# A pad of 128 bytes at the right end of SBUF in a fused attention and two-layer kernel

## Chip, cores and metric

The kernel runs on one core of one Trainium2 chip. The metric is the time of one execution on the device in microseconds. Where several executions were timed, the median stands with the lowest and the highest.

## What is computed

Three steps follow each other. The attention works over the channels (256 by 256 scores for each of 2 batches), so that its product with `v` can be folded into the weights of the next layer. Two feed-forward layers follow, with 1536 and 2048 hidden units, over 12032 tokens of 256 channels, all in float32.

```python
B, N, C = (2, 6016, 256)
qn = q / (np.linalg.norm(q, axis=1, keepdims=True) + 1e-06)
kn = k / (np.linalg.norm(k, axis=1, keepdims=True) + 1e-06)
s = kn.transpose(0, 2, 1) @ qn / tau
a = softmax(s)                       # over the last axis, plus 1e-9 in the sum
x = (v @ a).reshape(B * N, C)
x = (sigmoid(x @ w_gate) * (x @ w_val)) @ w_out      # 256 -> 1536 -> 256
h = x @ w_in                                         # 256 -> 2048
return (h - np.tanh(h)) @ w_out2                     # 2048 -> 256
```

## The kernel before

Every float32 operand is kept as two halves, a rounded high part and the rest (`split`, line 91), and each product is three matmuls: high by high, high by low, low by high (`prod`, line 415, whose matmuls are lines 419, 420 and 421). The first operand of a matmul is the weight that is loaded into the array (128 by 128), the second is the data that stream through it (up to 512 columns).

At the start the scores of batch 0 are summed up over all its rows (lines 324 to 346), while a side stream converts the first layer's weights from a raw layout (`convert`, line 95: load, three steps on VectorE, a rescaling on GpSimd, a cast on ScalarE, a subtraction). After the softmax, `aw_block` (line 285) multiplies the attention matrix into these weights; the result is `aw`. From then on a list of units, sorted by hand-set due times (lines 632 to 641), is run in order. A unit of the first layer (`s1_mm`, line 426) makes gate and value `ps` from `vhl` and `aw`; its second half (`part_c`, line 501) adds `y` from `hl` and `wo`. A unit of the second layer (`s2_mm`, line 448) makes `h` from `yhl` and `wi`, and its second half adds `o` from `hl` and `wv`. The tokens are cut into 24 tiles: 22 of 512 and 2 of 384, the last of each batch. The scores of batch 1 are computed in between by a list of side steps (line 625).

SBUF is filled from both ends by pools that open and close like a stack on each side. On the left lie `base` (constants, `wo`, `aw`), `vp` (`vraw`, `vhl`), then `sp` for the attention of batch 0, and after `sp` is closed `mp` (`yhl`, `sg`, `hl`), `cst` or later `m2` and `cst2` (staging of the other weights, and the second layer's work tiles), `qp`, `qp2` and `yp`. On the right lie `wp` (line 81: the six `wgv` tiles) and `stg` (line 82: raw tiles and `x` tiles of their conversion); both are closed in turn, and `w2p` (line 406) takes the place with eight `wi` and eight `wv` tiles. The pools have `reuse_waits="tile"`: a new tile waits for the users of just those old tiles whose bytes it takes.

The places that matter here, in bytes of a partition, as the layout of the kernel before has them:

| tiles | side | from | to | start modulo 512 |
|---|---|---|---|---|
| `ident`, `ones` | left | 16512 | 17536 | 128 |
| `wo` (6 of 4096) | left | 17632 | 42208 | 224 |
| `aw` (6 of 8192) | left | 42208 | 91360 | 224 |
| `vhl` | left | 95456 | 103648 | 224 |
| `sp`, all | left | 103648 | 153944 | 224 for its large tiles |
| `yhl`, in `mp` | left | 103648 | 111840 | 224 |
| `hl` (4 of 4096), in `mp` | left | 115936 | 132320 | 224 |
| last tiles of `cst` | left | 148704 | 156896 | 224 |
| last tiles of `cst2`, `qp`, `qp2` | left | 150752 | 163064 | 224 for the large ones |
| `stg`: raw tiles from 155616, 159712, 163808, 167904, then `x` tiles | right | 155616 | 180192 | 480 |
| `wp`: `wgv` (6 of 8192) | right | 180192 | 229344 | 480 |
| `w2p`: `wi`, `wv` (16 of 4096) | right | 163808 | 229344 | 480 |

All slices of these tiles that TensorE reads begin a multiple of 512 bytes after the tile's start.

Of the kernel before, what the change touches and what calls it, by code (L numbers as in the profile page):

```python
# [8 lines left out]
F32 = mybir.dt.float32  # L9
# [8 lines left out]
P = 128  # L18
# [39 lines left out]
def attn_moe_kernel(  # L58
# [18 lines left out]
    pp = ctx.enter_context(tc.tile_pool(name="pp", bufs=1, space=bass.MemoryType.PSUM))  # L77
    sctx, wctx, gctx, cctx = ExitStack(), ExitStack(), ExitStack(), ExitStack()
    vp = ctx.enter_context(tc.tile_pool(name="vp", bufs=1))
    sp = sctx.enter_context(tc.tile_pool(name="sp", bufs=1, reuse_waits="tile"))  # L80
    wp = wctx.enter_context(tc.tile_pool(name="wp", bufs=1, side="right", reuse_waits="tile"))
    stg = gctx.enter_context(tc.tile_pool(name="stg", bufs=1, side="right", reuse_waits="tile"))
# [450 lines left out]
    def side_load(r):  # L533
        if r < R:
            raw = qp.tile([P, 2, D], F32, tag="raw", bufs=2, name=f"raw1_{r}")
            for t, src in ((0, q), (1, k)):
                nc.sync.dma_start(raw[:, t, :], token_rows(src, 1)[:, r, :])
            q1["raw", r] = raw
# [86 lines left out]
    side = [side_open, lambda: side_load(0), lambda: side_load(1)]  # L625
# [105 lines left out]
```

## Time and profile before

| | us |
|---|---|
| median of 3 runs | 2364.32 |
| lowest and highest | 2363.01 and 2366.67 |
| the profiled execution's own time | 2363.61 |
| its span, first to last instruction | 2361.7 |
| TensorE busy in it | 2325.5 |

Some 1.9 us of the profiled execution lie outside the span. Times in the rows below are counted from the span's start. Matmuls overlap: the duration of one (about 390 ns for 512 columns) is longer than the distance from one start to the next, and it is this distance that sets the pace.

### The profile page before, as it was taken

The page shows a single profiled execution, that of the slowest core. Times are in us where ns is not written, and L with a number is a line of the kernel's source. Part 1 is how long each engine was busy: PE and PEld are TensorE (multiplying, and loading weights), DVE is VectorE, ACT ScalarE, POOL GpSimd, SP SyncE. Part 2 cuts the span into 40 slices and gives each one's busy share as a digit, 9 for nine tenths or more (in the row PEclk, how much of TensorE's full clock was granted, in tenths as well). Part 3 has the DMA queues.
Part 4 walks back from the last instruction along what each step waited for, and adds up shares of the span by engine and source line. Part 5 has one row for each costly group of instructions (what it writes and reads, how often), then busy time and mean ns, then how long its engine had stood idle before and what let it go on. Part 6 is the DMA issues. An engine that isn't in the chain of part 4 may idle for free.

```text
span 2361.7 us, 28761 instructions
## 1 busy us (share of the span) xinstructions
PE 2325.5 (98%) x10704; PEld 1953.9 (83%) x10704; DVE 1870.5 (79%) x2917; ACT 1563.2 (66%) x2808; POOL 118.3 (5%) x82
## 2 busy tenths in 40 slices
PE   8899999999999999999999999999999999999998
PEld 8777888888888888878889888888888888888887
DVE  7898787888888888888777778777787777777777
ACT  4456667676677766677666666666666666666667
POOL 4531000000000000000000000000000000000004
PEclk9999999999999999999999999999999999999999
DMA  8530000101101001000110000000000000000000
GB/s 296 217 116 18 28 18 27 36 14 36 36 19 36 22 33 36 18 16 27 63 54 1 16 18 1 18 18 1 18 10 10 18 10 10 18 1 16 10 1 16
DMA packets 37516, 81.53 MB, mean 35 GB/s; under 512 B 3840, under 2 KB 17152, under 8 KB 35840
## 3 DMA queue, kind: packets, MB, share of 16 engines
q1 hardware_dynamic: 29568, 61.09, 7.8%
q10 hardware_dynamic: 6912, 12.32, 1.4%
q0 software_dynamic: 896, 6.29, 0.6%
q8 instruction: 83, 1.36, 0.2%
q14 instruction: 57, 0.47, 0.1%
HBM read 61.08 MB, written 18.61 MB: 34 GB/s over the span
## 4 chain that ended last, share of the span: by engine, by line
PE 91%; DVE 5%; ACT 1%; issue 1%; DMA 1%; POOL 0%; ACTq 0%; SPq 0%; DVEq 0%; POOLq 0%
PE ps L420 11%; PE ps L419 11%; PE ps L421 11%; PE o L420 7%; PE o L421 7%; PE o L419 7%; PE h L420 7%; PE h L419 7%; PE h L421 7%; PE y L420 5%; PE y L421 5%; PE y L419 5%; DMA raw<-in_k_dram 1%; DVE hl L93 1%; DVE hl L498 0%
## 5 line engine op out<-in xcount | busy, mean ns | idle before, releaser
L467 DVE TENSOR_TENSOR d<-h,d 128x512 f32<-128x512 f32 (+1 forms) x368 | 251.7, 684 | 250.8 <-ACT d L463 250.5
L420 PE MATMUL ps<-vhl,aw 128*128 128x512 f32 (+1 forms) x1152 | 444.4, 386 | 0.8 <-DVE vhl L93 0.8
L419 PE MATMUL ps<-vhl,aw 128*128 128x512 f32 (+1 forms) x1152 | 444.3, 386 | 0.0
L421 PE MATMUL ps<-vhl,aw 128*128 128x512 f32 (+1 forms) x1152 | 443.9, 385 | 0.0
L496 ACT CAST hl<-s 128x512 fp32r<-128x512 f32 (+1 forms) x384 | 234.6, 611 | 302.8 <-DVE s L470 297.7
L462 ACT ACTIVATE u<-h 128x512 f32<-128x512 f32 (+1 forms) x384 | 226.3, 589 | 258.0 <-PE h L421 257.1
L468 DVE TENSOR_TENSOR u<-h,u 128x512 f32<-128x512 f32 (+1 forms) x368 | 251.2, 683 | 112.3 <-ACT big L466 112.2
L420 PE MATMUL o<-hl,wv 128*128 128x512 f32 (+1 forms) x768 | 297.6, 387 | 7.1 <-DVE hl L498 5.7
L420 PE MATMUL h<-yhl,wi 128*128 128x512 f32 (+1 forms) x768 | 296.5, 386 | 2.2 <-DVE yhl L93 2.2
L419 PE MATMUL o<-hl,wv 128*128 128x512 f32 (+1 forms) x768 | 296.4, 386 | 1.6 <-ACT hl L496 1.2
L419 PE MATMUL h<-yhl,wi 128*128 128x512 f32 (+1 forms) x768 | 296.1, 385 | 0.9 <-ACT yhl L92 0.9
L421 PE MATMUL o<-hl,wv 128*128 128x512 f32 (+1 forms) x768 | 296.3, 386 | 0.0
L421 PE MATMUL h<-yhl,wi 128*128 128x512 f32 (+1 forms) x768 | 296.1, 385 | 0.0
L470 DVE COPY_PREDICATED s<-big,d 128x512 f32<-128x512 int16 (+1 forms) x368 | 274.0, 745 | 12.5
L464 ACT ACTIVATE s<-u,c_b 128x512 f32<-128x512 f32 (+1 forms) x384 | 275.1, 716 | 3.3 <-DVE hl L498 3.3
L466 ACT ACTIVATE big<-u,c_m 128x512 bf16<-128x512 f32 (+1 forms) x368 | 263.8, 717 | 0.0
L469 DVE SCALAR_TENSOR_TENSOR s<-s,u 128x512 f32<-128x512 f32 (+1 forms) x368 | 253.0, 687 | 12.6
L419 PEld LDWEIGHTS ps<-vhl,aw 128*128 128x128 f32 x1152 | 216.8, 188 | 41.8 <-DVE aw L93 0.4
L420 PEld LDWEIGHTS ps<-vhl,aw 128*128 128x128 f32 x1152 | 216.7, 188 | 41.8 <-DVE vhl L93 1.1
L421 PEld LDWEIGHTS ps<-vhl,aw 128*128 128x128 f32 x1152 | 216.7, 188 | 41.6
L498 DVE TENSOR_TENSOR hl<-s,hl 128x512 fp32r<-128x512 f32 (+1 forms) x370 | 249.4, 674 | 0.1
L443 DVE TENSOR_TENSOR sg<-ps,sg 128x512 f32<-128x512 f32 (+1 forms) x288 | 194.0, 674 | 61.4 <-PE ps L421 60.1
(149 smaller groups left out, 3729.4 us busy)
## 6 DMA issues: line engine op xcount, KB each, us to landing
vraw<-in_vT_dram SPq DMA_DIRECT2D x22, 512.0 KB, 3.7
out_dram<-out ACTq DMA_DIRECT2D x44, 256.0 KB, 2.0
raw<-in_q_dram SPq DMA_DIRECT2D x48, 128.0 KB, 2.1
raw<-in_k_dram SPq DMA_DIRECT2D x48, 128.0 KB, 2.2
raw_wgv<-in_wgv_dram SPq DMA_DIRECT2D x12, 512.0 KB, 6.5
wgv_d<-wgv POOLq DMA_DIRECT2D x6, 1024.0 KB, 8.6
wb<-wgv_d SPq DMA_DIRECT2D x6, 1024.0 KB, 4.8
raw<-in_q_dram SPq DMA_DIRECT2D x11, 512.0 KB, 5.3
```

The lines of the kernel that those rows point to most:

```text
L419: mm(ps[:, :n], wh, xh, start=first and j == 0, stop=False)
L420: mm(ps[:, :n], wh, xl, start=False, stop=False)
L421: mm(ps[:, :n], wl, xh, start=False, stop=last and j == m - 1)
L462: nc.scalar.activation(u, H, AF.Square)
L464: nc.scalar.activation(s, u, AF.Square, scale=C_S, bias=c_b[:, 0:1])
L466: nc.scalar.activation(big, u, AF.Relu, bias=c_m[:, 0:1])
L467: nc.vector.tensor_sub(d, H, d)
L468: nc.vector.tensor_mul(u, H, u)
L469: nc.vector.scalar_tensor_tensor(s, s, C_D, u, op0=ALU.add, op1=ALU.mult)
L470: nc.vector.copy_predicated(s, big.bitcast(I16), d)
L496: nc.scalar.copy(hl[:, 0, :n], x)
L498: eng.tensor_sub(hl[:, 1, :n], x, hl[:, 0, :n].bitcast(F32))
```

## The change

One more pool of one tile is opened on the right side, ahead of every other pool of that side, and stays open to the end. Its tile has 128 partitions by 32 float32 values, which is 128 bytes in each partition. Nothing writes or reads it. It takes the bytes from 229216 to 229344, and all pools of the right side begin 128 bytes further left: `stg` from 155488, `wp` from 180064 and `w2p` from 163680.

```diff
@@ -77,6 +77,8 @@
     vp = ctx.enter_context(tc.tile_pool(name="vp", bufs=1))
+
+    ctx.enter_context(tc.tile_pool(name="pad", bufs=1, side="right")).tile([P, 32], F32, name="pad")
     sp = sctx.enter_context(tc.tile_pool(name="sp", bufs=1, reuse_waits="tile"))
     wp = wctx.enter_context(tc.tile_pool(name="wp", bufs=1, side="right", reuse_waits="tile"))
     stg = gctx.enter_context(tc.tile_pool(name="stg", bufs=1, side="right", reuse_waits="tile"))
```

## Rows read from the trace of the kernel before

**Rows 1.** The page, part 1: busy us, share of span, instructions of each engine.

```profile
PE 2325.5 (98%) x10704; PEld 1953.9 (83%) x10704; DVE 1870.5 (79%) x2917; ACT 1563.2 (66%) x2808; POOL 118.3 (5%) x82
```

**Rows 2.** The page, part 4: the chain that ended last, by engine and line.

```profile
PE 91%; DVE 5%; ACT 1%; issue 1%; DMA 1%; POOL 0%; ACTq 0%; SPq 0%; DVEq 0%; POOLq 0%
PE ps L420 11%; PE ps L419 11%; PE ps L421 11%; PE o L420 7%; PE o L421 7%; PE o L419 7%; PE h L420 7%; PE h L419 7%; PE h L421 7%; PE y L420 5%; PE y L421 5%; PE y L419 5%; DMA raw<-in_k_dram 1%; DVE hl L93 1%; DVE hl L498 0%
```

**Rows 3.** Busy time by stretches: length, engines with instructions, clock, DMA share, GB/s.

```profile
0.00:60.00 60.00, 49.42 (x380) 48.31 (x381) 44.89 (x51) 26.93 (x31) 27.65 (x22) 1.00 0.84 297
60.00:120.00 60.00, 51.38 (x248) 42.60 (x247) 50.57 (x86) 26.82 (x46) 34.20 (x24) 0.91 0.56 207
120.00:200.00 80.00, 74.70 (x315) 59.65 (x314) 73.59 (x123) 41.48 (x75) 28.31 (x14) 0.98 0.29 99
...
1000.00:1200.00 200.00, 198.20 (x919) 168.10 (x918) 159.21 (x255) 139.92 (x250) 0.00 (x0) 1.00 0.11 37
...
1400.00:1600.00 200.00, 200.00 (x884) 165.64 (x884) 148.46 (x227) 129.44 (x232) 0.00 (x0) 1.00 0.04 14
...
2300.00:2340.00 40.00, 36.04 (x172) 31.12 (x171) 34.63 (x63) 32.92 (x69) 18.07 (x15) 0.96 0.04 14
2340.00:2362.00 22.00, 15.82 (x80) 14.00 (x78) 14.50 (x28) 13.12 (x29) 10.09 (x9) 0.87 0.05 18
```

**Rows 4.** Timeline of TensorE from 1500 us: start and duration in us, line, tiles.

```profile
1501.60 0.39 PE L419 MATMUL ps<-vhl,aw 128*128 128x512 f32 x1
...
1504.32 0.39 PE L419 MATMUL y<-hl,wo 128*128 128x512 f32 x1
...
1508.39 0.39 PE L419 MATMUL h<-yhl,wi 128*128 128x512 f32 x1
...
1511.12 0.39 PE L419 MATMUL ps<-vhl,aw 128*128 128x512 f32 x1
```

**Rows 5.** TensorE's matmuls by shape: count, busy us, mean ns, idle before.

```profile
L420 PE MATMUL ps<-vhl,aw 128*128 128x512 f32 x1056 | 412.2, 390 | 0.8 <-DVE vhl L93 0.8
...
L420 PE MATMUL o<-hl,wv 128*128 128x512 f32 x704 | 275.0, 391 | 4.0 <-DVE hl L498 4.0
L420 PE MATMUL h<-yhl,wi 128*128 128x512 f32 x704 | 274.5, 390 | 0.2 <-DVE yhl L93 0.2
...
L420 PE MATMUL y<-hl,wo 128*128 128x512 f32 x528 | 205.7, 390 | 1.1 <-DVE hl L498 1.1
...
L420 PE MATMUL h<-yhl,wi 128*128 128x384 f32 x64 | 22.0, 344 | 1.9 <-DVE yhl L93 1.9
```

**Rows 6.** Weight loads of TensorE by shape, in the same columns.

```profile
L419 PEld LDWEIGHTS ps<-vhl,aw 128*128 128x128 f32 x1152 | 216.8, 188 | 41.8 <-DVE aw L93 0.4 <-ACT vhl L92 0.2
...
L420 PEld LDWEIGHTS h<-yhl,wi 128*128 128x128 f32 x768 | 144.5, 188 | 29.5 <-DVE yhl L93 2.9
...
L571 PEld LDWEIGHTS norm<-nacc,ones 128*128 128x128 f32 x2 | 0.4, 188 | 0.1
```

**Rows 7.** Conversions of weights in the first 220 us, by shape, in the same columns.

```profile
L116 ACT CAST wgv<-x_wgv 128x512 fp32r<-128x512 f32 x12 | 6.9, 618 | 0.0
...
L117 DVE TENSOR_TENSOR wi<-x_wi,wi 128x512 fp32r<-128x512 f32 x8 | 5.5, 685 | 0.2
...
L116 ACT CAST wo<-x_wo 128x512 fp32r<-128x512 f32 x6 | 3.6, 621 | 0.2 <-DVE x_wo L130 0.2
...
L117 DVE TENSOR_TENSOR wo<-x_wo,wo 128x512 fp32r<-128x512 f32 x6 | 3.8, 682 | 0.0
```

**Rows 8.** The page, part 6: DMA issues with count, KB each, us to landing.

```profile
raw_wgv<-in_wgv_dram SPq DMA_DIRECT2D x12, 512.0 KB, 6.5
wgv_d<-wgv POOLq DMA_DIRECT2D x6, 1024.0 KB, 8.6
...
raw_wo<-in_wo_dram SPq DMA_DIRECT2D x6, 512.0 KB, 5.4
```

**Rows 9.** Waits in the first 200 us: who for whom, us, times, longest.

```profile
POOL x_wgv L109 <- DMA raw_wgv<-in_wgv_dram: 22.0, 4, 18.1
```

## The prediction

> **What bounds the kernel now.** I read the page's busy shares first: TensorE (PE) is at work for 2325.5 of 2361.7 us [rows 1], so 36.2 us of the span are all that it leaves idle. The chain that ended last says the same: 91% of it is PE, spread over the four kinds of matmul `ps`, `y`, `h` and `o` in about the ratio of their counts [rows 2]. The table by stretches says where the idle time lies [rows 3]: 10.6, 8.6 and 5.3 us in the first 200 us (together 24.5), 1.8 us between 1000 and 1200, and 4.0 and 6.2 us at the end; the sum is 36.5. Between 200 and 1000, and from 1200 to 2300, PE is never idle, at a granted clock of 1.00, which is the 2.4 GHz level. So the time is the count of matmuls times their pace, plus some 36 us of start, joint and tail. The pace comes out of the timeline: 12 matmuls of the first layer from 1501.60 to 1504.32 us are 2.72 us, 226.7 ns each; 12 of the second layer from 1508.39 to 1511.12 are 2.73 us, 227.5 ns each [rows 4]. A time in that view is good to 0.01 us, so to 0.8 ns in each of these. At 2.4 GHz 512 columns alone are 213.3 ns; every matmul costs some 13.4 ns more than its columns.
>
> **What the change does, part by part.** The pad is never written or read. It adds no instruction, DMA or wait. What it moves are addresses: all that lies at the right end slides down by 128 bytes, that is `wp` (weights `wgv`), `stg` (the staging of their conversion) and, later in the same place, `w2p` with `wi` and `wv`. Everything on the left stays. Four things could follow.
>
> *Waits.* A tile that takes an old tile's bytes waits for that tile's users. Tiles on the right slide together, so their overlaps with each other stay. Across the two sides I went through the layout in the section on the kernel. `sp` ends at 153944, the lowest tile of `stg` begins at 155616 and then 155488: still apart. The later left tiles reach 163064, `w2p` begins at 163808 and then 163680: still apart. Where tiles of `cst`, `cst2` and `qp` do lie on the old `stg` slots, each touches the same slots for a shift of 128: the slots' borders move from 159712 to 159584 and from 163808 to 163680, and no tile begins or ends between those. So no wait comes or goes: 0 us.
>
> *Pace of the second layer's matmuls.* This is the one large term. `h` and `o` are 6 groups of 704 matmuls of 512 columns and 6 of 64 of 384 [rows 5], 4608 in all; each nanosecond on one is 4.6 us on the end, since nothing hides PE. What a weight tile's place does to it is to be read by offset. All moving tiles begin at 224 modulo 512, `aw` and `wo` also, `wi` and `wv` at 480, and every slice is a multiple of 512 bytes further. So weights and moving data stand 0 apart modulo 512 in the first layer and 256 apart in the second; after the change the second's stand 128 apart. The trace has both old distances side by side, and they have one pace (226.7 and 227.5 ns, above) and one duration: 390, 390, 390 and 391 ns for `ps`, `y`, `h`, `o` [rows 5]. The weight loads are at 188 ns for both [rows 6], and at 188 ns also for `ones`, whose tile begins at 128 modulo 512, where the loads of `norm` take it from [rows 6]. A distance of 128 itself the trace does not show for these matmuls, so the price is bounded from both sides by what the rows allow: the whole surplus of 13.4 ns gone, or as much again added, 4608 x 13.4 ns = 62 us either way. I take 0, as the nearest rows (distances 0 and 256, and a weight load at a third phase) agree within their reading.
>
> *Conversions on the right.* ScalarE's cast from right to right (`wgv`) takes 618 ns, from left to left (`wo`) 621; VectorE's subtraction takes 682 ns into a left tile (`wo`) and 685 into a right one (`wi`) [rows 7]. So the side shows 3 ns, at most 0.1 us over the 28 tiles. I take 0.
>
> *DMAs on the right.* 12 loads of `raw_wgv` at 6.5 us from issue to landing, while a load of the same size into a left tile takes 5.4 [rows 8]; GpSimd waits 22.0 us for them, in 4 waits [rows 9]. They fall in the first 120 us, where the DMA engines are 84% and 56% busy and PE idles for 19.2 us [rows 3]. A 128-byte shift leaves counts and sizes alone. If it made each of them cheaper or dearer by the 1.1 us between the two rows, 12 x 1.1 = 13 us of landing time would move. Most of that lies beside work that PE has: it idles for 16% of these 120 us, and 16% of 13 is 2.1 us. I bound the effect on the end at 2.1 us either way and take 0, since nothing in size or count changes. The six stores of `wgv` to DRAM at 8.6 us [rows 8] read from the right too; their data is wanted again only after 1000 us, so a percent more or less costs nothing. [...]
>
> The sum is 0 us against the profiled execution, 2363.6 us with 2361.7 of span. The median of the runs shown is 2364.3 and lies 0.7 above it; the predicted time is that median.
>
> **Rivals.** *The reads collide, and the pad parts them* (faster). A weight load runs beside the matmul ahead of it, and both read SBUF. If the 13.4 ns are lost to that, and by an address pattern that repeats every 256 bytes, then 0 and 256 are one and the same case, which is why the rows agree, and 128 is the opposite one. All of layer two's surplus gone is -62 us: 2302. VectorE, at 79% [rows 1], would not be the bound yet. For it speaks that the surplus exists and that all pairs in this kernel stand at one distance modulo 256. Against it speaks that the surplus is the same within 1 ns in all four kinds, whatever lies between the tiles. [...]
>
> *The pad brings a collision that was not there* (slower). The same mechanism with the other sign: distances of 0 modulo 256 are the good case now, and at 128 each weight load of `wi` and `wv` costs the stream as much again. PE has no slack in its steady stretches to cover it: +62 us, 2426. Even a twelfth of that per matmul, 1.1 ns, would be 5 us and visible. For it speaks only that the distance is untried; against it the same rows.
>
> *The pad does not move anything*, for example if an unused tile gets no place. Then the program is the one of before, and the time too. It falls in with the forecast.
>
> **How the numbers follow.** No change of time: 0.81, the third rival in it. Faster by a collision that goes: 0.11. Slower by one that comes: 0.08. Likeliest is no change: 2364.3 us. What a measurement of this kernel can tell from no change is about 0.2%, 4.7 us. The three runs of before span 3.7 us, the start may move by 2.1 us either way, and other runs may scatter as widely again: the range is 2359 to 2370. It leaves out the two collision cases, 0.19 in all. A case of a ns per matmul would fall just at its ends.
>
> **What would show it.** Right: the four groups `ps`, `y`, `h`, `o` stay at 390 ns and 12 matmuls of `h` and `o` at 2.73 us; 36 us of idle PE in the same stretches; 188 ns of weight load. Wrong: a pace of `h` and `o` that differs from that of `ps` and `y`, which would be a collision of either sign; or the same pace with more idle PE in the first 120 us, which would be the loads. If the number of instructions or of PE's waits differs, my reading of the layout is wrong.

## The result

The changed kernel takes 2394.53 us (median of 4 runs, 2393.52 to 2396.89) against 2364.23 us before (the three runs of before and one more): a ratio of 1.013, with a 95% interval of 1.0115 to 1.0145. It is 30 us slower. The forecast was no change, with 2370 as the upper end.

The profiled execution of the changed kernel took 2394.82 us, 2392.7 of them span, 31.0 more than before. The page's busy times of the engines, part 1:

```profile
PE 2355.3 (98%) x10704; PEld 1953.9 (82%) x10704; DVE 1869.9 (78%) x2917; ACT 1575.8 (66%) x2808; POOL 119.1 (5%) x82
```

The counts of instructions are those of before [rows 1]. PE is busy 29.8 us longer and idle for 37.4 us in place of 36.2. So the loss is not in waiting: the same matmuls take longer. The stretches of the changed kernel, in the columns of [rows 3]:

```profile
0.00:60.00 60.00, 49.24 (x382) 48.03 (x383) 43.80 (x51) 26.83 (x31) 28.72 (x22) 1.00 0.84 300
60.00:120.00 60.00, 49.87 (x246) 40.75 (x245) 51.21 (x88) 26.97 (x46) 34.59 (x24) 0.91 0.54 204
...
1400.00:1600.00 200.00, 200.00 (x868) 162.92 (x867) 149.59 (x228) 133.75 (x235) 0.00 (x0) 1.00 0.04 14
```

From 1400 to 1600 us PE is never idle and its granted clock is 1.00, as before, but 868 matmuls fit in where 884 did [rows 3]. In the first 120 us PE idles 1.7 us longer than before. Which matmuls are slower is in the list by shape, whose columns are those of [rows 5] (the change moved every line by 2, so 421, 422 and 423 are the old 419, 420 and 421):

```profile
L423 PE MATMUL ps<-vhl,aw 128*128 128x512 f32 x1056 | 413.8, 392 | 0.0
L421 PE MATMUL ps<-vhl,aw 128*128 128x512 f32 x1056 | 413.7, 392 | 0.0
L422 PE MATMUL ps<-vhl,aw 128*128 128x512 f32 x1056 | 412.5, 391 | 0.8 <-DVE vhl L95 0.8
L422 PE MATMUL o<-hl,wv 128*128 128x512 f32 x704 | 279.6, 397 | 3.5 <-DVE hl L500 3.4
L421 PE MATMUL o<-hl,wv 128*128 128x512 f32 x704 | 279.3, 397 | 1.1 <-ACT hl L498 1.1
L421 PE MATMUL h<-yhl,wi 128*128 128x512 f32 x704 | 278.9, 396 | 0.0
L423 PE MATMUL o<-hl,wv 128*128 128x512 f32 x704 | 278.7, 396 | 0.0
L422 PE MATMUL h<-yhl,wi 128*128 128x512 f32 x704 | 277.7, 394 | 0.2 <-DVE yhl L95 0.2
L423 PE MATMUL h<-yhl,wi 128*128 128x512 f32 x704 | 277.6, 394 | 0.0
L423 PE MATMUL y<-hl,wo 128*128 128x512 f32 x528 | 207.1, 392 | 0.0
L421 PE MATMUL y<-hl,wo 128*128 128x512 f32 x528 | 206.7, 392 | 0.0
L422 PE MATMUL y<-hl,wo 128*128 128x512 f32 x528 | 205.6, 389 | 1.0 <-DVE hl L500 1.0
```

Summed over the three lines, `h` has 834.2 us here and 823.0 in the same view of before, `o` 837.6 and 823.7, `ps` 1240.0 and 1236.0, `y` 619.4 and 616.6. Of before, [rows 5] show one line of each kind; the others of `h` and `o` are these:

```profile
L421 PE MATMUL o<-hl,wv 128*128 128x512 f32 x704 | 274.4, 390 | 0.0
L419 PE MATMUL o<-hl,wv 128*128 128x512 f32 x704 | 274.3, 390 | 1.2 <-ACT hl L496 1.2
L419 PE MATMUL h<-yhl,wi 128*128 128x512 f32 x704 | 274.3, 390 | 0.0
L421 PE MATMUL h<-yhl,wi 128*128 128x512 f32 x704 | 274.2, 389 | 0.0
```

The differences are +11.2, +13.9, +4.0 and +2.8 us, together 31.9, which covers the 31.0 between the spans. A duration here is the distance to the next start plus 162 ns (the median of the matmuls of 512 columns in either trace, nearly all within 160 to 164), so a longer duration is a slower pace. The second layer, whose weights the pad moved, carries 25 us of it: 5.9 ns on each of its 4224 matmuls of 512 columns. The first layer, where nothing moved, carries 7. The timeline of PE shows how that can be, where the kernel goes from the first layer to the second and back (start and duration in us):

```profile
1503.90 0.40 PE L422 MATMUL o<-hl,wv 128*128 128x512 f32 x1
1504.14 0.40 PE L423 MATMUL o<-hl,wv 128*128 128x512 f32 x1
1504.38 0.40 PE L421 MATMUL ps<-vhl,aw 128*128 128x512 f32 x1
...
1506.46 0.39 PE L421 MATMUL ps<-vhl,aw 128*128 128x512 f32 x1
...
1507.14 0.39 PE L421 MATMUL y<-hl,wo 128*128 128x512 f32 x1
...
1510.77 0.39 PE L422 MATMUL ps<-vhl,aw 128*128 128x512 f32 x1
1511.00 0.40 PE L423 MATMUL ps<-vhl,aw 128*128 128x512 f32 x1
1511.23 0.40 PE L421 MATMUL o<-hl,wv 128*128 128x512 f32 x1
...
1512.63 0.39 PE L421 MATMUL ps<-vhl,aw 128*128 128x512 f32 x1
```

From 1511.00 to 1512.63 there are 7 matmuls at 233 ns. After a stretch of the second layer, the first layer's 9 matmuls from 1504.38 to 1506.46 still go at 231 or 232 ns, and only the 3 from there to 1507.14 are back at 227 ns, the pace of [rows 4]. The first layer is slowed by what ran ahead of it, for some matmuls, and then falls back into step by itself. And the last matmul ahead of the second layer, at 1511.00, is long already (232 ns to the next start), though its own weights are `aw`: the weights that are loaded while it runs are `wv`. Counted in the trace from 200 to 2290 us, the 293 matmuls of the first layer with 512 columns under which a weight of the second layer is loaded go at 232.3 ns from start to start, and those in the same place of the kernel before at 226.9. That is some 1.6 of the first layer's 7 us; the rest lies in the matmuls after such a stretch, of which the first goes at 233.7 ns on average, the fourth at 231.0 and the tenth at 226.7 (226.8, 226.6 and 226.7 in the kernel before).

### The profile page after: what moved, and what is told of

It reads as the page before. It is cut to its first block, busy times and chain, and to the rows that moved or that the text cites. A ratio compares the mean times of both kernels' runs of the same rounds, so it can differ in the third digit from the quotient of the medians.

```text
span 2392.7 us, 28761 instructions
## 1 busy us (share of the span) xinstructions
PE 2355.3 (98%) x10704; PEld 1953.9 (82%) x10704; DVE 1869.9 (78%) x2917; ACT 1575.8 (66%) x2808; POOL 119.1 (5%) x82
## 4 chain that ended last, share of the span: by engine, by line
PE 92%; DVE 4%; DMA 1%; ACT 1%; issue 1%; POOL 0%; ACTq 0%; DVEq 0%; SPq 0%; POOLq 0%
PE ps L423 11%; PE ps L421 11%; PE ps L422 11%; PE o L422 7%; PE o L423 7%; PE o L421 7%; PE h L421 7%; PE h L422 7%; PE h L423 7%; PE y L423 5%; PE y L421 5%; PE y L422 5%; DMA raw<-in_k_dram 1%; PE qk L225 0%; PE qk L227 0%
## 5 line engine op out<-in xcount | busy, mean ns | idle before, releaser
L422 PE MATMUL o<-hl,wv 128*128 128x512 f32 (+1 forms) x768 | 301.8, 393 | 6.6 <-DVE hl L500 5.1
L421 PE MATMUL o<-hl,wv 128*128 128x512 f32 (+1 forms) x768 | 301.2, 392 | 1.4 <-ACT hl L498 1.1
L422 PE MATMUL h<-yhl,wi 128*128 128x512 f32 (+1 forms) x768 | 299.6, 390 | 2.1 <-DVE yhl L95 2.1
L421 PE MATMUL h<-yhl,wi 128*128 128x512 f32 (+1 forms) x768 | 300.8, 392 | 0.9 <-ACT yhl L94 0.9
L423 PE MATMUL o<-hl,wv 128*128 128x512 f32 (+1 forms) x768 | 300.4, 391 | 0.0
L423 PE MATMUL h<-yhl,wi 128*128 128x512 f32 (+1 forms) x768 | 299.4, 390 | 0.0
```

Source lines behind the costliest of these rows:

```text
L421: mm(ps[:, :n], wh, xh, start=first and j == 0, stop=False)
L422: mm(ps[:, :n], wh, xl, start=False, stop=False)
L423: mm(ps[:, :n], wl, xh, start=False, stop=last and j == m - 1)
```

## Experiments

The theory formed on the result is that of the rival that said slower: a weight load slows the matmul beside it, depending on how far apart in SBUF the weights and the data that stream start. The runs below were each timed once, beside the kernel before on the same chip (2364.95, 2364.10, 2362.43 and 2364.26 us in the four groups of runs); such single times of one kernel differ by some 4 us, so smaller differences are not read. An inserted line moves the line numbers of the matmuls by one (420, 421 and 422), in the kernel with two pads by two.

### Does the place count, or the distance?

Four kernels place the pad differently. The first makes it 256 bytes:

```diff
+    ctx.enter_context(tc.tile_pool(name="pad", bufs=1, side="right")).tile([P, 64], F32, name="pad")
```

> The pad on the right is 256 bytes instead of 128. Theory A (distance): what counts is how far the start of a weight tile lies from the start of the moving tile, modulo 256; distance 0 is good and 128 bad. Then the second layer is back at distance 0: about 2364 us, h and o at 390 ns as in the kernel before. Theory B (place): any other place of wi and wv than that of before costs: about 2394 us, h and o at 395 to 397 ns.

Measured: 2361.92 us beside 2364.95, `h` 389 to 390 ns, `o` 390 to 391. Theory B, by which any other place costs, falls. The second kernel puts 128 bytes at the left end:

```diff
+    ctx.enter_context(tc.tile_pool(name="padl", bufs=1)).tile([P, 32], F32, name="padl")
     base = ctx.enter_context(tc.tile_pool(name="base", bufs=1))
```

> The pad of 128 bytes lies at the left end, so everything on the left moves by 128 (moving tiles, aw, wo) and the right stays. Theory A (distance): the second layer is at distance 128 again, the first at 0: about 2394 us, h and o at 395 to 397 ns, ps and y at 390 to 392, as after the change. Theory C (start of the weights): a weight tile that starts at 96 modulo 256 is bad by itself: then ps and y are slow (396) and h and o fast (390), also some 2394 us; the groups tell them apart, not the time.

Measured: 2398.33 us. It is again the second layer that is slow, though it was the first one's weights that moved. From the list by shape:

```profile
L420 PE MATMUL ps<-vhl,aw 128*128 128x512 f32 x1056 | 414.1, 392 | 0.0
...
L421 PE MATMUL o<-hl,wv 128*128 128x512 f32 x704 | 279.6, 397 | 3.5 <-DVE hl L499 3.5
...
L420 PE MATMUL h<-yhl,wi 128*128 128x512 f32 x704 | 278.9, 396 | 0.0
```

The third has both pads at once, 128 bytes at either end.

> A pad of 128 bytes at both ends: all tiles start at 96 modulo 256, all distances are 0. Theory A (distance): about 2364 us, all four groups at 390 ns. Theory C (start of the weights): both layers slow, about 2364 + 2 x 30 = 2424 us. Theory B (place): about 2394 us or more.

Measured: 2364.89 us beside 2364.95. All four groups are back at 389 to 391 ns, with every large tile at another place than before:

```profile
L421 PE MATMUL ps<-vhl,aw 128*128 128x512 f32 x1056 | 412.2, 390 | 0.0
...
L422 PE MATMUL o<-hl,wv 128*128 128x512 f32 x704 | 275.5, 391 | 4.0 <-DVE hl L500 4.0
...
L422 PE MATMUL h<-yhl,wi 128*128 128x512 f32 x704 | 274.5, 390 | 0.2 <-DVE yhl L95 0.2
...
L422 PE MATMUL y<-hl,wo 128*128 128x512 f32 x528 | 205.7, 390 | 1.1 <-DVE hl L500 1.1
```

Two shifts that cost 30 and 33 us alone cancel, which of the three theories only the distance explains. The fourth has the 128 bytes between the first layer's weights and the tiles that stream:

```diff
+    ctx.enter_context(tc.tile_pool(name="padm", bufs=1)).tile([P, 32], F32, name="padm")
     vp = ctx.enter_context(tc.tile_pool(name="vp", bufs=1))
```

> A pad of 128 bytes in the middle of the left side, between the weights aw, wo and the tiles that stream. No weight tile moves; vhl, hl, yhl move by 128, so both layers are at distance 128. Theory A (distance): all four groups slow, 395 to 397 ns; with some 5.7 ns on each of 9360 matmuls about 2364 + 53 = 2417 us. Theory C (start of the weights): no weight moved, 2364 us.

Measured: 2412.49 us, 47.5 above the kernel before beside it, where theory A had said 53; all four groups are slow, with no weight tile of the two layers moved:

```profile
L420 PE MATMUL ps<-vhl,aw 128*128 128x512 f32 x1056 | 417.3, 395 | 0.0
...
L421 PE MATMUL o<-hl,wv 128*128 128x512 f32 x704 | 279.2, 397 | 3.2 <-DVE hl L499 3.1
...
L421 PE MATMUL h<-yhl,wi 128*128 128x512 f32 x704 | 278.0, 395 | 0.2 <-DVE yhl L94 0.2
...
L421 PE MATMUL y<-hl,wo 128*128 128x512 f32 x528 | 208.5, 395 | 0.9 <-DVE hl L499 0.9
```

So theory A holds in all four: what counts is the distance between the start of a weight tile and that of the tile that streams, modulo 256. Theory C, the weights' own start, falls in the last three. In this last kernel the first layer stands 384 apart modulo 512 and the second 128, with the same effect within 2 ns (395 to 397); as 0 and 256 agreed before, at 390 and 391 ns [rows 5], the pattern repeats at 256.

### The second layer alone

The pad is opened after the first stage, so that staging and conversion of `wgv` stay where they were:

```diff
     wctx.close()
+    ctx.enter_context(tc.tile_pool(name="pad", bufs=1, side="right")).tile([P, 32], F32, name="pad")
     w2p = ctx.enter_context(tc.tile_pool(name="w2p", bufs=1, side="right", reuse_waits="tile"))
```

> The pad of 128 bytes is opened only after the first stage, just before the second layer's weights are placed; the staging tiles and wgv stay at their places of before. If the whole loss lies in the pace of the second layer and what carries over from it: about 2394 us, h and o at 394 to 397 ns, while the 72 matmuls that read wgv go back to their durations of before. If the loads and conversions on the right had a part in it: less, down to 2392 us.

Measured: 2394.77 us, that of the full change. Loads, conversions and `wgv` have no measurable part in it. One part of the expectation did not come: the 72 matmuls that read `wgv` took 436, 420 and 413 ns on their three lines, against 446, 424 and 419 before and 433, 414 and 414 in the changed kernel. The differences add up to some 0.5 us; why they are there stays open.

### All distances in steps of 32 bytes

Pads of other sizes on the right, in otherwise the same kernel.

> The pad on the right is 32 bytes; the second layer stands 224 (that is, -32) apart modulo 256. Distance counts modulo 256, the runs so far show; open is the shape between 0 and 128. Theory A1 (two streams that sweep the same 256 bytes, cost grows with the distance up to 128): about a quarter of the 30 us, 2372 us. Theory A2 (0 alone is good): about 2394 us, h and o at 396 ns. Theory A3 (128 alone is bad): 2364 us.

> The pad on the right is 64 bytes; distance 192 (-64) modulo 256 in the second layer. A1 (cost grows with the distance): about half of the 30 us, 2379 us. A2 (0 alone is good): about 2394 us. A3 (128 alone is bad): 2364 us. If another distance than 0 lets the weight load in with less than the 13.4 ns, the time is below 2360 us.

> The pad on the right is 96 bytes. Pads of 32, 64, 128 and 192 gave +25, +8, +30 and +30 us, 256 none: no growth with the distance, and no mirror. Theory G (a weight row that is off by an odd number of 32 bytes collides more than one off by 64): about 2389 us, as with 32. Theory H (the cost grows from 64 to 128): between 2372 and 2394, about 2383 us. Below 2364 us it would be a distance that is better than 0.

> The pad on the right is 160 bytes, between 128 and 192, which both cost 30 us. If the cost is smooth there: about 2394 us. Theory G: about 2389 us or more. Below 2364 us it would be a better distance than 0.

> The pad on the right is 192 bytes; distance 64 modulo 256 in the second layer, the mirror of a pad of 64. If the sign of the distance does not count, the time is that of the pad of 64 within 4 us; A1 2379 us, A2 2394 us, A3 2364 us. If the order of the two reads counts, the two differ.

> The pad on the right is 224 bytes, 32 short of a whole 256. Theory G: about 2389 us, as with 32. If the cost falls smoothly from 192 to 256: about 2379 us. If the order of the two reads counts (pads of 64 and 192 differ by 22 us), it need not be that of the pad of 32.

| pad, bytes | time, us | above the kernel before beside it |
|---|---|---|
| 32 | 2388.90 | +24.8 |
| 64 | 2371.87 | +7.8 |
| 96 | 2399.42 | +37.0 |
| 128 (the change) | 2394.53 | +30.3 |
| 160 | 2395.11 | +32.7 |
| 192 | 2393.63 | +29.5 |
| 224 | 2392.38 | +30.0 |
| 256 | 2361.92 | -3.0 |

Every distance but 0 costs. None of the three shapes that I had written down fits: the cost does not grow with the distance (a pad of 32 costs three times as much as one of 64), 0 is not alone against one flat level (64 lies in between), and 128 is not the only bad one. Theory G, by which an odd number of 32 bytes is worse, fits 32 against 64 but not 192, which costs as much as 160 and 224. Theory H, by which 96 lies between 64 and 128, falls too: 96 costs most of all. With a pad of 160 the smooth course came true, with one of 224 it did not (2379 us expected). The signs are not mirrored: 64 and 192 stand 64 bytes apart either way and differ by 22 us. Why 64 is the mild one stays open; the list by shape of that run says only where it pays:

```profile
L421 PE MATMUL h<-yhl,wi 128*128 128x512 f32 x704 | 277.3, 394 | 0.2 <-DVE yhl L94 0.2
...
L420 PE MATMUL h<-yhl,wi 128*128 128x512 f32 x704 | 275.9, 392 | 0.0
...
L422 PE MATMUL h<-yhl,wi 128*128 128x512 f32 x704 | 273.7, 389 | 0.0
```

Two of three matmuls pay, and line 422 does not. And no distance in steps of 32 made the kernel faster than 0 does. In the trace of before, matmuls of 512, 384 and 256 columns follow each other at 227, 174 and 120 ns (medians from 200 to 2290 us), 0.418 ns a column from the first to the last, which leaves some 13 ns beyond the columns; the times show no distance that wins them back.

### A matmul's own weights, or the next load

A weight load starts some 3 ns after the matmul ahead of it does and takes 188 of the 227 ns to the next start (medians of the trace of before), so either a matmul's own weights could matter or the load for the next one. Two kernels tell them apart by moving just one half of the weights in two of the eight `wi` tiles. In the first the low half lies 128 bytes off:

```diff
-        wi_t.append(w2p.tile([P, 2, CH], F32R, name=f"wi{c}"))
+        wide = w2p.tile([P, 2, CH + (32 if c < 2 else 0)], F32R, name=f"wilow{c}" if c < 2 else f"wi{c}")
+        wi_t.append(wide[:, :, :CH])
```

> No pad at the end; in two of the eight wi tiles (wilow0, wilow1, used by 4 of 16 units of each token tile) the low half lies 128 bytes further from the high half, so that the high half is at distance 0 and the low half at 128. A product runs as high x high, high x low, low x high (lines 420, 421, 422). The load of the low half runs during the matmul of line 421. Theory N (the load of the next weights collides with the stream that runs meanwhile): the matmuls of line 421 are long, those of 422 only by what carries over. Theory O (a matmul's own weights count): those of line 422 are long, those of 421 stay at 390 ns. The time by either: 24 x 4 x 2 = 192 matmuls at 6 to 14 ns and what carries over, 2365 to 2370 us.

Measured: 2363.67 us, no difference from the 2364.10 beside it and below the 2365 to 2370 expected. The longer matmuls of the list below add up to some 2 us, which single runs cannot show. The list by shape of that run:

```profile
L422 PE MATMUL h<-yhl,wilow 128*128 128x512 f32 x176 | 69.8, 397 | 0.0
L421 PE MATMUL h<-yhl,wilow 128*128 128x512 f32 x176 | 69.7, 396 | 0.2 <-DVE yhl L93 0.2
L420 PE MATMUL h<-yhl,wilow 128*128 128x512 f32 x176 | 68.7, 390 | 0.0
```

Line 421 works with the high half, which is in place, while the low half is being loaded, and it is long (396 ns). Line 422 works with the low half and is long too. So N explains 421 and needs a carry-over for 422; O alone would have left 421 at 390. Whether misplaced weights also cost the matmul that works with them something of their own, this run cannot separate from a carry-over. The second kernel has the high half off in its place (the view begins 32 elements into the wide tile):

```diff
+        wide = w2p.tile([P, 2, CH + (32 if c < 2 else 0)], F32R, name=f"wihigh{c}" if c < 2 else f"wi{c}")
+        wi_t.append(wide[:, :, (32 if c < 2 else 0) :])
```

> The counterpart of the run with the low half off: in two of eight wi tiles (wihigh0, wihigh1) the high half is at distance 128 and the low half at 0. In a product the loads of the high half run during the matmul ahead of line 420 (that of another product or line 422) and during line 420; the load of the low half runs during line 421. Theory N with carry-over (the load collides with the stream under way): line 420 is long, being the first whose stream meets a load of the high half inside the product, 421 at most by carry-over, and 422 long inside a unit, where the next high half is loaded. Theory O (a matmul's own weights count, with carry-over to the next): 420 and 421 are long from their own weights, 422 by what carries over. Between units the two differ: by N the last matmul of the unit ahead, which still streams with other weights, is the first long one (232 ns to the next start in place of 227); by O it is at 227.

Measured: 2369.69 us beside 2364.26. The timeline of PE around one such unit:

```profile
1507.73 0.39 PE L421 MATMUL y<-hl,wo 128*128 128x512 f32 x1
1507.96 0.40 PE L422 MATMUL y<-hl,wo 128*128 128x512 f32 x1
1508.19 0.40 PE L420 MATMUL h<-yhl,wihigh 128*128 128x512 f32 x1
1508.43 0.40 PE L421 MATMUL h<-yhl,wihigh 128*128 128x512 f32 x1
1508.67 0.39 PE L422 MATMUL h<-yhl,wihigh 128*128 128x512 f32 x1
1508.90 0.39 PE L420 MATMUL h<-yhl,wihigh 128*128 128x512 f32 x1
1509.13 0.40 PE L421 MATMUL h<-yhl,wihigh 128*128 128x512 f32 x1
1509.37 0.39 PE L422 MATMUL h<-yhl,wihigh 128*128 128x512 f32 x1
1509.60 0.39 PE L420 MATMUL y<-hl,wo 128*128 128x512 f32 x1
```

To the nanosecond the trace has 227, 232, 241, 240, 231, 232, 233, 231, 226 from each start to the next. The first long one is the matmul of `y` at 1507.96: its own weights, `wo`, are at distance 0, and what runs under it is the load of a high half that is 128 off. That is theory N, and it is no single case: over the trace from 200 to 2290 us the 74 matmuls of 512 columns that run just ahead of such a unit go at 231 to 233 ns, and the others outside these units at 227.0 on average. The matmul at 1508.43 is at 240 although the low half that is loaded under it is in place: a disturbed stream seems to carry over into the next, or its own high half counts as well. The matmul at 1509.37 parts the two: its own low half and the load under it are both in place, and it is at 231 (84 such matmuls in the trace are at 230.9 on average), so there is a carry-over. At 1509.60 the pace is back.

Why the address of a load matters to the matmul beside it was not shown: the runs have times and addresses, and no row has the reads themselves.

## Why the prediction was wrong

**What bounds the kernel, and waits, conversions, loads**: right. PE is the bound before and after, the instructions are the same in number, and PE's idle time moved by 1.2 us, so no wait of weight came or went. (The idle times that the prediction adds up come to 36.5 us in place of 36.2 because its last stretch ends 0.3 us behind the span; nothing rests on it.) The cast of `wgv` is at 618 ns as in [rows 7], a load of `raw_wgv` lands in 6.4 us against 6.5 in [rows 8], and the kernel with the pad at `w2p` alone has the full loss (2394.77 us).

**Pace of the second layer's matmuls**: this step failed, the one that the prediction itself called the large term. It set the price at 0 because the distances 0 and 256 had one pace and a weight load at a third phase had the usual 188 ns. Both were weak witnesses. 0 and 256 are one case when the pattern repeats at 256, as it does; the text of the faster rival says just that, and the layout showed every large tile at 224 modulo 256. What stood for two samples was one, and an agreement of one sample with itself was taken as evidence. The 188 ns say nothing either: the second row of [rows 6] is at 189 ns in the changed kernel:

```profile
L422 PEld LDWEIGHTS h<-yhl,wi 128*128 128x128 f32 x768 | 145.2, 189 | 32.6 <-DVE yhl L95 2.7
```

The load keeps its time within 1 ns, and the stream beside it pays: 394 to 397 ns for `h` and `o` in place of 389 to 391, some 25 us, and 7 more in the first layer. I looked for the cost at the wrong one of the two. The sign of being wrong that the prediction named, a pace of `h` and `o` that differs from that of `ps` and `y`, is the one that came.

**The slower rival**: right in its sign and in what it makes the loss depend on, the distance at which the second layer's weights are loaded, with 0.08 too small a chance, and mis-sized. That two reads collide was its guess at the cause, and no run shows it. It put the price at the whole surplus of 13.4 ns on each of the 4608; measured are 5.9 ns on those of 512 columns. It missed a second term: the first layer, which no tile of the change touches, pays 6.8 us, because its last matmul ahead of a stretch of the second layer has that stretch's first weight load beside it (232.3 ns in place of 226.9), and by carry-over behind the stretch.

**The faster rival**: it had the same period and the opposite sign; seven other distances were run and none is faster.

**The surplus and the DMAs**: the 2.4 GHz and the 13.4 ns behind the 62 us fit the trace of before: 0.418 ns a column is 2.39 columns per ns, and some 13 ns stay beyond the columns. As a bound they held: a weight load beside the stream cost at most 37.0 us over the kernel with the second layer off (a pad of 96), and 47.5 us with both layers off, depending on nothing but addresses. As a gain they were not reached at any distance in steps of 32 bytes, with a weight load for every matmul: the steady pace of some 227 ns remained the best. For the DMAs 0 was right as far as the rows go: the stores land in 8.5 us in place of 8.6, but the loads of `raw_wo`, whose place did not move, also went from 5.4 to 4.9.

## What to carry to other kernels

When float32 data stream through TensorE with a new weight load for every matmul, keep the starts of weight tiles and streaming tiles equal modulo 256 bytes, as far as this one kernel shows (389 to 391 ns a matmul there, 394 to 397 with 128 bytes between), and look at this again after every small tile that is added to a pool: 32 bytes in the wrong place were worth 1% here. Before a cost is set at nothing because two cases agree, ask whether they differ in what the change alters. And the cost of a moved tile is to be read at every instruction that runs beside the one that moved, not only at that one.

## What was not expected of the hardware

A weight load slows the matmul under way beside it by its address alone: 227 ns from start to start with distance 0 modulo 256 in the trace of before, 228 to 241 ns (232.8 on average) with 128 in that of the changed kernel, while the load itself stays at 188 to 189 ns. A disturbed stream hands its disturbance on: after the last misplaced load, in the timeline from 1504.38 us, 9 matmuls whose own tiles are all in place were still at 231 or 232 ns on average, and then the stream fell back to 227; in the kernel with the high half off it came back after two matmuls (226 ns at 1509.60). What decides between the two is not settled, nor is the shape of the map, in which a pad of 64 bytes costs 8 us and one of 96 costs 37.
